# Hashed attention and two feed-forward layers on one core: constant-tile matmuls put into TensorE's order, and a new table of order and engines

## The chip, the core and the metric

The kernel runs on one core of a Trainium2 chip. The core has five instruction streams that run side by side and meet at semaphores: TensorE (PE; its weight loads are listed as PEld), VectorE (DVE), ScalarE (ACT), GpSimd (POOL), and SyncE (SP), which here only issues DMAs. Each engine takes its instructions strictly in the order in which they are written. The metric is the device time of one execution in microseconds (us). TensorE's clock has two levels, 1.2 and 2.4 GHz; the profile gives the granted clock as a share of the upper one, so 0.5 is the lower level, and a number between is a mix of both over a stretch.

## The reference

```python
# attention: batch 2, 8 heads, 768 positions, head size 64, 6 hash bits
q_bits, k_bits = (q @ proj > 0), (k @ proj > 0)      # 6 bits make a bucket
mask   = q_bucket[:, :, :, None] == k_bucket[:, :, None, :]
scores = where(mask, q @ k.T / 8, -1e9)
attn   = softmax(scores)                             # exp(s - max) / (sum + 1e-9)
x = (attn @ v) -> [1536 tokens, 512]
# first layer, 512 -> 2048 -> 512
h = x @ w_in;  g = where(h >= 1, h, where(h <= -1, 0, (h + 1)**2 / 4));  x = g @ w_out
# second layer, same sizes, other weights
h = x @ w_in2; g = h - tanh(h);  y = g @ w_out2
```

The weights arrive as 64-bit floats, everything else as 32-bit floats.

## The kernel before, in words

**Attention** is cut into 96 softmax tiles (48 for each batch), one for 128 query rows of a head against all 768 keys. For a tile, PE makes the scores in two pairs of matmuls (`emit_s`, L435 and L439) into the PSUM tile `ss` (in the first quarter also `mm`); the second pair adds the hash bits in such a way that unequal buckets sink. DVE takes the row maximum (`soft`, L453) and two tiny numbers from it (L456), ACT takes the exponential (L457). The result `p` is split into two 16-bit halves `phl` (a copy, L462, on ACT; a subtraction, L463 on POOL or L464 on DVE), transposed by a DMA into `pt` (L468), or, for three of the head pairs, on PE (`turn`, L512), and multiplied with `v` on PE (`pv`, L550 and L540). The hash bits come from small matmuls into the PSUM tile `pb` (`q_bits` L340 and L341, `k_bits` L326 and L327, `first_k` L309 and L310), which DVE reads (L344, L330, L313). `pb` also takes the spread-out reciprocals of the softmax sums (`scale_l`, L490), the transposes in later tiles, and the largest `v` (L355). There is one `pb`, a PSUM bank of 512 columns of which the kernel uses 384; in the second half of the tiles there is also one `ss` alone.

**The layers** work on 128x512 pieces of weights. A piece is loaded (512 KB, `w<-in_w`), narrowed from 64 to 32 bits (ACT L662; DVE L663, L664, L666, all into `wr`), and split into a high part `wh` (a copy, L227) and a low part `wl` (a subtraction, L233 on POOL or L234 on DVE). Three matmuls of 384 columns each (high x high, high x low, low x high) make up one product (`mats`, L709, 3072 matmuls in all). The results `tmp` are activated (L728 to L733), split again into `gh` and `gl`, and summed in `accs` (L750 to L759). The matmuls of the layers begin during attention, as soon as the first four head pairs are there, and go on alone once attention is over.

**Order and engine.** The code hands some 2000 operations to a `Plan`, each with the engines that can do it: `copy_hi` (L227) may be ACT or DVE, `sub_lo` (L233 POOL, L234 DVE) POOL or DVE, and so on. The table `SCHEDULE`, a packed list of numbers, says in which order the operations are written and which engine takes each (`unpack`, `emit`). Within an engine that order is final. Waits between engines are put in by the framework from the tiles that an instruction reads and writes. Costs that stand beside an operation in the code are not used when the kernel is built.

Of the kernel before, what the change touches and what calls it, by code (L numbers as in the profile page):

```python
# [19 lines left out]
SCHEDULE = (  # L20
    "c-rk&Yj9Q775>)V`<#8wx#vD}-#3q&<lf}oyvT#_N&-RvdCAil1PddT3ZkGwkO&M9d6ic|XsrkYXm|(|Q40e|oeH8I+wqS-svT#n){Zl6wbSX3PJgxgMuCcf"
    "B!E??*~!dVXPv#jyI$W~8?gq`A$cKu5SYj{4i0EbAgcZ~5IWCO3g#2%!3`URZt4bfU5gYsijYhuL=gGo5N9?6M#W5*348F+pnBV&`%q*gvDWRE!slF(tHa?>"
    "l{moKyosO}{ylMWLx($xSv%qmA<iIRq`<<`ixV16jz`1<XKe^}v~m=O9KqBXNj^cgGSBXBQa$=g$o^Fk^cmPkZ$N!cZLKKP{I#e|3GgA@sIRXFr6`>Sij&p6"
    "3VkOgYFI%zV)0mY3^_=aBT<UN5Kt8G7X^?A=lip=@&Z|$BNFkZJjJ0x<_@^y@tj=Lx$+T<Mx7BvZNY6q)Id1w2}y+D4B#IHc|0oz+1c=tCk%Ig!0-RSk!8OR"
    "#|OU`c>i4<kzqI!EC5HmKmu>&c{DQ{#2q@!YVABIdX`7{=_pQf77B%&_-paUf5ve0qfe3_n&uxH3!NW-Xu^^AUY_y0Tu5KDjK}g2e=us~A}0qThCqx*5#lV!"
    "oMe$@x$<0OC{wLS2%(S})cnS@N8zi1*L(L|9h2S6<NBu?9+hFI(+L7hhiOF+HbdBEXmS`f>2o;$0cN}41RUvf6}Nbi$x9OkFZ;#hmoe!@rZIsR__5ezfl;~R"
    "?_}W-j75W-`Pr^b4d7nB6UcgsoLE_717ueydsKm~C`-wg<<jDl+ETovCBWw(uCYfRU~JYbJa|9x&xm~wn>jX4!_Eyf{SUMjn7X<NE3uwUUdiBEb!nyRA}w{I"
    "b@}2}j9G+wJO*O{=1b^j=i#UZaag>FqX+Txc6P}41V;`_v|-;q+P6pFLwM^s@SpNa&%Dkr{`Ml?VnV!`?T86>=^|b;UQ^ZfO8}g^;X382)<DnOIE+KqQT)A~"
    "jL-0?Z2!x?za6qZwf4(BZ4%F!*rnl5Iuv1^=J*)+$jkBWJIsZ5e&c@Itt$78H}EE2w{XFD?d@8_0K1^$S0r8~&R;o2ICBm!sZ^X|FPuEdahxdpy!vq*gzY<E"
    "AGAGf*w5Nrd)afQ!rbGO<}T7DNgdeiP79Y%^f}0W1e0iuq}|Jb7<-a~mOQ<fwJ2AX;0Y}DZf;T4y=Xmi!X_dUkd+dB^>u_6@Ks<d7#1wUV;m2&R<x+r;76A5"  # L30
    "iPhll6>zzhF=1mJG1J2gl~cP~0YB7_59M>qIsZNv%6<o{L!p_Z{K~$-(rUz)R8GxpDdjo56fB71M1ZKa@J_&6)fnfV`*>_{S@z)ECa_5Hln5(h>CuX}1;s_G"
    "Q1UFqr7=Q}x{#+&*K>judby?<vR>wSJUOQ3%6G*z*=XlWBy<>IFFZomqdrwjX$}`pa_(Tt0l>$+Zsr!uX@|MPf%R6g)1n0O^No0+nFmv{92uo3(|9OD1kNcF"
    "`<j}Wu&ZX=hssJm)v5q9rj)+tVH0OfBou4ow6SB67%d9T0y3t>iJD3A(5P#c5ivl=q)B`XmW*dLcQONWWTPD6Lg4=0x@|o>V~A<#1MkK5se_sgr)J}a!c(nH"
    "HYcHvF<vET>|SkrD;w<;5DN*62G586aQ!@cNL}5_s22~^iPZyE-H%oMXD&CejOl1a6|l&7^l_$ocF80B#|N-;o`ap=J{RZAGg}XDRYhX##HKCVw;bQH=_uE*"
    "fvs-`TZ?^Y)7NlqHyA&Wsk)yW!C|*~a0i?R4mkH4_SSQOlY0UuAm2W|3%)mT<kFGjM=l(D=BW1S^EfZ?O8cRE&q5sFe7|b$zi!)mg5mfD^B7ctpFbzgomGT5"
    "bNXij4$k(n7f!%FZXc7+64WSZ*EPkLHqnN?d-$2%T%5)!E}mhEx;xl0V%zX<m5cVxIIyLGZ{D~U8+U`&3#KAMJMc8NBL*3<Hc14rJ}i;7y<nSIl|LV18|M$<"
    "$hu93vg2;7&e<1Tll{~R>~bz&u{FBoIF=tp@(7;P*FoE;Lh<3kRcdC?0??DRycJmHYBgK@_J+kR(pa-_As%0;M&yEJ8s@dHZ1pZ#F6MgJB1Ni2S$KSh5A)%9"
    "SeP!%+2DE5z-))2)(Q=L{)|VUQZsE%OrzPe1(r3<TIvpRJTZf{*kU>?V$GN*;lVM@a6-)lb0%rfG%(h@tprZG8&lN8Twhl=-p|+oYx?N^m}-u6Q%w_Sl0A`O"
    "ymc4Gsrkr8LC}bqyonmw<eB#}G~d@eofgC7{2pM6t?h#)=9*%drOHF1eyDy225AH94Nhv>_v;7N7ls?<(pfHjrRfseTPz((cfW+AuR2j1hgB^tm=${3P<5|5"
    "T%n_&fHRQHQQbWX5%wkoq^m*K!C9@zQDc$vMZI~zb!I2jpo^G!WI!rj=?H282ZWCd3aCv!8xC-jD`$0|Cb?jmx<il}6;4?q%hC>{tyGZ(En(CkSt#=>h~?%Y"  # L40
    "EeJ&;P@f!zL5ZRP4T)skgk(c)Vn71bNP32=-V^UrHrW3FTsebM$jmsK+Y@S=s^TFyCOSr0SulsEFl=P;bfb8Pk!)--hSU$9lrZY8ftE4G>^BptPpJ}}s)c9Y"
    "6N?}uCh1)D6VFruYGQ0OyJI*|-cWATp>!ZCVMvz@N!3)RpmI2+Kgz}eqsL+FC{&F?<?s=eBS)go(4l>hRbD~l9Y}EB;|3B=R89c9i`A5aN>R~(#xzPBF<@|U"
    "f24{^lm&@IMIpw3$IB~`DplKx(tVIZB3aTeiBw@(VG&q<AuCXU&dn#vCM1!F6e1i0f?<RMkzf%1Xeba2sg{l`uh*+gWbnFdWd0ncX}Z+(hmmm@nM<Ieo&lj!"
    "DAZ1vP^?r{tvbAtucyB%Ynk)vU)?Izo6LZU4o%1Vjj*qe*Kw``<?>VFio)oQeOL9L+jkXD(XK<fqW_Y8oyls4RDNZEnN(h>8<e^RqeGKXUKP|vsFuqzvf6nC"
    "s1q&ym-35%U4H8N7s1pr->3uN@-gLn=HhWJz?JX%6+bV#`?;WB7L>Q0S<tyCt_j^W*!Uto86;hN9(t(^%-jyp@rx|8Ewe$Wr3@DxupPeku5at2uLzglsdIfd"
    "@d!6QPF;bs|Iak^uJ3xV>Dy@`eS=}8TLYzD0`@xGyLwme>Rq>~_kCrqP**qE?lw^Bffe6aucw|{OW&Q5LAT=Qx9r+TUoZUE;lkHrGX3va(&MwYh5Pgk(xr<J"
    "UAjp(*@n7rDs`LF)S3Ns?Wyip8FhtzJ6p~TB27KEv|CZXvDtJ3ir*-N)B|t3J#o7zB<evf>AKMLr6f}iDAbjm-9x3D=P`93m2S2d+**}WPhIZndUhLn%a=Lb"
    "Gr6m0&#`Z}t+$TXm9BG<x~uIngmfM8X576Vz|B-o=W)3qz<&S=KC)c"
)


# [65 lines left out]
def lsh_attention_moe_kernel(ctx: ExitStack, tc: tile.TileContext, qT, kT, vR, projR, eye, w1, w2, w3, w4, out, nbits):  # L117
    nc = tc.nc
    B, H, D, S = qT.shape
# [689 lines left out]
    def pump(first):  # L809

        while True:
            n, p = ahead
            if n < NW and (room if raw[n] else n < p + len(WR) and free(n)):
                w_load(n)
                ahead[0] += 1
            elif p < n and free(p) and p - len(WH) < first:
                w_narrow(p)
                w_split(p)
                ahead[1] += 1
            else:  # L820
                return
# [86 lines left out]
```

## Time and profile before

| | us |
|---|---|
| median of 3 runs | 814.67 |
| lowest, highest run | 814.52, 821.42 |
| profiled execution, its own time | 816.48 |
| its span, first to last instruction | 814.7 |
| PE busy in the span | 751.9 (92%) |
| DVE, ACT, POOL busy | 555.3, 517.4, 269.7 |
| mean granted clock of PE | 0.969 |

So 1.8 us of the profiled execution lie around the span. Busy time is the union of an engine's instructions; a PE that is busy at the lower clock does half the work.

### The profile page before, as it was taken

What the parts mean: (1) busy time and instruction counts of PE and PEld (TensorE: products, weight loads), DVE (VectorE), ACT (ScalarE), POOL (GpSimd) and SP (SyncE); (2) the same over time, 40 slices, a digit from 0 to 9 for tenths busy, and PEclk for the clock granted to TensorE, in tenths of its full rate; (3) what the DMA queues carried; (4) which work ended last, traced back from release to release, by engine and by line L of the source; (5) the groups of instructions that cost most, each with busy time, mean ns of one, the idle gap of its engine ahead of it and who ended that gap; (6) DMA issues with size and microseconds to landing.
All of it is one profiled execution on the core that took longest, in us unless ns stands there. A gap on an engine that the chain in (4) does not pass through costs nothing.

```text
span 814.7 us, 12098 instructions
## 1 busy us (share of the span) xinstructions
PE 751.9 (92%) x4344; PEld 686.9 (84%) x4344; DVE 555.3 (68%) x950; ACT 517.4 (64%) x846; POOL 269.7 (33%) x197
## 2 busy tenths in 40 slices
...
GB/s 180 221 210 214 155 173 134 224 203 218 223 205 110 258 217 191 188 171 185 188 199 178 205 142 272 189 180 66 65 66 65 65 56 62 66 67 62 65 39 78
DMA packets 163724, 123.35 MB, mean 151 GB/s; under 512 B 126800, under 2 KB 133712, under 8 KB 163664
## 3 DMA queue, kind: packets, MB, share of 16 engines
...
q8 instruction: 34, 0.56, 0.3%
...
HBM read 71.96 MB, written 19.92 MB: 113 GB/s over the span
## 4 chain that ended last, share of the span: by engine, by line
PE 55%; DVE 4%; ACT 3%; DMA 3%; issue 1%; DVEq 0%; ACTq 0%; POOL 0%; POOLq 0%
PE mm L709 49%; PE pv L550 3%; DMA w<-in_w 2%; PE ss L435 1%; PE ss L439 1%; DVE sm L453 1%; ACT p L457 1%; DVE wr L666 1%; DVE wr L663 1%; DVE wr L664 0%; DMA pt<-phl 0%; DVE accs L759 0%; DVE phl L464 0%; PE pb L490 0%; ACT wh L227 0%
## 5 line engine op out<-in xcount | busy, mean ns | idle before, releaser
L233 POOL TENSOR_TENSOR wl<-wr,wh 128x512 fp32r<-128x512 f32 x85 | 113.4, 1340 | 369.5 <-ACT wh L227 360.6
L227 ACT ACTIVATE wh<-wr 128x512 fp32r<-128x512 f32 x144 | 89.7, 625 | 93.3 <-PE mm L709 82.1
L709 PE MATMUL mm<-xh,wh 128*128 128x384 f32 x512 | 138.7, 341 | 7.0 <-DVE tmp L730 3.9
L709 PE MATMUL mm<-gh,wh 128*128 128x384 f32 x512 | 138.1, 340 | 3.6 <-DVE accs L757 1.7
L709 PE MATMUL mm<-xl,wh 128*128 128x384 f32 x512 | 136.4, 336 | 0.8 <-POOL xl L233 0.8
L709 PE MATMUL mm<-gh,wl 128*128 128x384 f32 x512 | 135.8, 336 | 0.1
L709 PE MATMUL mm<-xh,wl 128*128 128x384 f32 x512 | 135.7, 336 | 0.0
L709 PE MATMUL mm<-gl,wh 128*128 128x384 f32 x512 | 135.7, 335 | 0.0
L457 ACT ACTIVATE p<-ss,sm 128x768 f32<-128x768 f32 x78 | 77.1, 988 | 43.8 <-DVE sm L456 41.2
L709 PEld LDWEIGHTS mm<-xh,wh 128*128 128x128 f32 x512 | 92.5, 189 | 12.4 <-DVE tmp L730 5.1
L709 PEld LDWEIGHTS mm<-gh,wh 128*128 128x128 f32 x512 | 92.3, 188 | 7.5 <-DVE tmp L730 2.9
L453 DVE TENSOR_REDUCE sm<-ss 128x1 f32<-128x768 f32 x82 | 78.2, 953 | 29.1 <-PE ss L439 25.5
L709 PEld LDWEIGHTS mm<-xl,wh 128*128 128x128 f32 x512 | 93.5, 189 | 1.8 <-POOL xl L233 1.8
L709 PEld LDWEIGHTS mm<-gh,wl 128*128 128x128 f32 x512 | 93.2, 188 | 0.4 <-POOL wl L233 0.4
L709 PEld LDWEIGHTS mm<-gl,wh 128*128 128x128 f32 x512 | 93.4, 188 | 0.0
L709 PEld LDWEIGHTS mm<-xh,wl 128*128 128x128 f32 x512 | 93.3, 189 | 0.0
L463 POOL TENSOR_TENSOR phl<-p,phl 128x768 f16<-128x768 f32 x35 | 59.1, 1688 | 70.3 <-ACT phl L462 65.8
L759 DVE TENSOR_TENSOR accs<-mm,accs 128x768 f32<-128x768 f32 x45 | 42.8, 954 | 55.5 <-PE mm L709 55.2
L234 DVE TENSOR_TENSOR wl<-wr,wh 128x512 fp32r<-128x512 f32 x59 | 42.9, 727 | 52.2 <-ACT wh L227 52.0
L227 ACT ACTIVATE gh<-tmp 128x768 fp32r<-128x768 f32 x64 | 53.9, 844 | 33.1 <-DVE tmp L730 18.2
L234 DVE TENSOR_TENSOR gl<-tmp,gh 128x768 fp32r<-128x768 f32 x53 | 51.8, 979 | 29.8 <-ACT gh L227 29.7
L462 ACT ACTIVATE phl<-p 128x768 f16<-128x768 f32 x69 | 57.8, 838 | 4.0 <-DMA pt<-phl 2.9
(162 smaller groups left out, 1192.0 us busy)
## 6 DMA issues: line engine op xcount, KB each, us to landing
...
```

What stands on the lines that cost most here:

```text
L227: ways = [("A", ca, lambda: A.activation(dst, src, AF.Copy)), ("V", cv, lambda: V.tensor_copy(dst, src), 1)]
L233: op([("G", cg, lambda: G.tensor_tensor(dst, src, hi.bitcast(F32), op=ALU.subtract)), ("V", cv, lambda: V.tensor_tensor(dst, src, hi.bitca ...
L234: ("V", cv, lambda: V.tensor_tensor(dst, src, hi.bitcast(F32), op=ALU.subtract), 1)], reads, writes)
L435: T.matmul(ps[:, c, 0:SH], Aq[n][:, i * 128:(i + 1) * 128], a[:, c * SH:(c + 1) * SH], start=True, stop=False)
L439: T.matmul(ps[:, c, 0:SH], Bq[n][:, i * 128:(i + 1) * 128], b_[:, c * SH:(c + 1) * SH], start=False, stop=True)
L453: one("V", 870.0, lambda: V.tensor_reduce(z[:, 0:1], s, axis=AX.XY, op=ALU.max), cell, [c])
L457: one("A", 970.0, lambda: A.activation(halves(p), s, AF.Exp, bias=z[:, 2:3], scale=z[:, 1:2], accum_out=LS[lm][:, lk:lk + 1]), cell + [c], ...
L462: hi = [("A", 730.0, lambda: A.activation(hl[:, 0:S], p, AF.Copy)), ("V", 470.0, lambda: V.tensor_copy(hl[:, 0:S], p), 1)]
L463: lo = [("G", 1600.0, lambda: G.tensor_tensor(hl[:, S:2 * S], p, hl[:, 0:S], op=ALU.subtract)), ("V", 870.0, lambda: V.tensor_tensor(hl[:, ...
L550: T.matmul(ps[j * 64:j * 64 + 64], v[:, kc, a, j, :], PT[n[j]][:, c * KC + kc, :], start=(kc == 0 and i == 0), stop=(kc == KC - 1 and i == 2))
L709: T.matmul(ps[:, s + hf, 0:SH], m[:, kc * 128:(kc + 1) * 128], y[:, hf * SH:(hf + 1) * SH], start=(kc == 0 and i == 0), stop=(kc == 3 and ...
L759: one("V", 870.0, lambda: V.tensor_tensor(a, ps, a, op=ALU.add), [pc], c)
```

## The change

Three things change. First, a constant 128x128 tile `warm` of 16-bit floats is made once on DVE (a copy of the unit matrix, as the fifteenth or so of DVE's instructions), and 65 new operations `spin` of four matmuls each multiply it with itself into the columns 384 to 511 of `pb`, which nothing reads. They have no reads or writes in the plan, and each of the 260 matmuls has a weight load of its own. Second, the table is another one: order and engines differ in nearly every place. Third, a cost beside L490's operation changes, which is not used.

```diff
+SPINS = 65
 SCHEDULE = (
...
+    warm = sb.tile([128, 128], F16, name="warm")
+    WT = PB[0][:, 3 * 128:4 * 128]
...
+    V.tensor_copy(warm, unit)
...
-            one("PE", 406.0, fn, [("rb", 0), ("rb", 1)], ["pb"])
+            one("PE", 640.0, fn, [("rb", 0), ("rb", 1)], ["pb"])
...
+    def spin():
+        for _ in range(4):
+            T.matmul(WT, warm, warm, start=True, stop=True)
+
+    for _ in range(SPINS):
+        one("PE", 300.0, spin, [], [])
+        plan.rows[len(plan.ops) - 1] = 0.7
     plan.emit()
```

Counted in the two built programs, the instructions of the engines move so: ACT 752 to 653, DVE 952 to 1040, POOL 202 to 214, PE 260 matmuls more and otherwise the same. The copies (L227) go from ACT to DVE: `wh` 46 of 144, `gh` 19 of 64, `aq` 7, `bq` 4, `xh` 5, and `phl` (L462) 5. Of these 86 copies 52 stand behind the last row maximum (L453) in DVE's order. Of the subtractions for `phl`, 14 go from DVE to POOL; of those for `gl` 7 go from DVE to POOL, and of those for `xl` 13 come from POOL to DVE. Of the 260 new matmuls, 120 stand ahead of the 29th softmax tile, 60 more ahead of the 48th, 80 between the 48th and the 53rd, and none later. In the new program's waits, the first matmul of a spin waits in 21 places for the DVE or ACT instruction that reads what PE wrote into `pb` before, and 11 reads of `pb` by DVE or ACT wait for a spin that stands between PE's write and the read.

**PE's order where batch 0 goes over into batch 1.** `gh,aq` is the last score tile of batch 0 (the 48th), `ak,aq` the first of batch 1. Before:

```order
L439 MATMUL ss_154<-gl_131,bq_78 128x384 x2
L709 MATMUL mm_153<-xh_137,wh_119 128x384 x2
L709 MATMUL mm_153<-xl_145,wh_119 128x384 x2
L709 MATMUL mm_153<-xh_137,wl_122 128x384 x2
L435 MATMUL ss_154<-gh_126,aq_75 128x384 x2
L439 MATMUL ss_154<-gl_131,bq_78 128x384 x2
L435 MATMUL ss_154<-ak_71,aq_76 128x384 x2
L439 MATMUL ss_154<-bk_73,bq_79 128x384 x2
L490 MATMUL pb_156<-unit,rb_102 128x128 x3
L435 MATMUL ss_154<-ak_71,aq_76 128x384 x2
```

The changed order has the following there (line numbers are 9 higher from here on: L444 and L448 are the scores, L718 is the layers' matmul).

```order
L448 MATMUL ss_154<-gl_131,bq_78 128x384 x2
L718 MATMUL mm_153<-xh_136,wh_119 128x384 x2
L718 MATMUL mm_153<-xl_144,wh_119 128x384 x2
L718 MATMUL mm_153<-xh_136,wl_122 128x384 x2
L718 MATMUL mm_153<-xh_137,wh_119 128x384 x2
L718 MATMUL mm_153<-xl_145,wh_119 128x384 x2
L718 MATMUL mm_153<-xh_137,wl_122 128x384 x2
L444 MATMUL ss_154<-gh_126,aq_75 128x384 x2
L448 MATMUL ss_154<-gl_131,bq_78 128x384 x2
L872 LDWEIGHTS warm
L872 MATMUL pb_156<-warm 128x128
```

Twelve layer matmuls instead of six now stand ahead of the last score tile of batch 0, and behind it 32 matmuls of the constant tile (the last two rows, 32 times over) ahead of the first tile of batch 1. Behind that tile stand 8 more, then L490, then 4 and, past the next hash bits, 8.

**PE's order early, around the hash bits of a query group.** The place is in the first dozen score tiles; `aq` into `pb` (L340 before, L349 now) are the hash bits, which DVE reads. Before:

```order
L439 MATMUL mm_152<-xl_148,bq_78 128x384 x2
L340 MATMUL pb_156<-aq_76,pw_65 128x384
L341 MATMUL pb_156<-aq_76,pw_66 128x384
L435 MATMUL mm_153<-xh_140,aq_75 128x384 x2
L439 MATMUL mm_153<-xl_148,bq_78 128x384 x2
L550 LDWEIGHTS v_0_85
```

Now:

```order
L444 MATMUL mm_153<-xh_140,aq_75 128x384 x2
L499 MATMUL pb_156<-unit,rb_102 128x128 x3
L448 MATMUL mm_153<-xl_148,bq_78 128x384 x2
L872 LDWEIGHTS warm
L872 MATMUL pb_156<-warm 128x128
```

Three more such pairs follow, one spin in all, and then the hash bits (L349 and L350). So a spin stands between L499, whose result ACT reads out of `pb`, and the hash bits: its first matmul waits for ACT's read. Two more spins follow L350, and DVE's read of the bits (L353) waits for one of them.

**DVE's order at the 61st row maximum.** `wr` is a weight piece being narrowed, `bq` the hash bits that a later score tile needs. Before:

```order
L453 TENSOR_REDUCE sm_94<-ss_154 128x1
L456 TENSOR_SCALAR sm_94<-sm_94 128x1 x2
L666 SCALAR_TENSOR_TENSOR wr_116<-w_1_112,wr_116 128x512
L481 TENSOR_SCALAR ls_101<-ls_101,vsm_90 128x6
L663 TENSOR_SCALAR wr_113<-w_0_111 128x512
L483 RECIPROCAL ls_101<-ls_101 128x6
L664 SCALAR_TENSOR_TENSOR wr_113<-w_0_111,wr_113 128x512
L234 TENSOR_TENSOR wl_120<-wr_116,wh_117 128x512
L666 SCALAR_TENSOR_TENSOR wr_113<-w_0_111,wr_113 128x512
```

Now:

```order
L462 TENSOR_REDUCE sm_94<-ss_154 128x1
L465 TENSOR_SCALAR sm_94<-sm_94 128x1 x2
L739 SCALAR_TENSOR_TENSOR tmp_134<-tmp_134,mm_153 128x768
L673 SCALAR_TENSOR_TENSOR wr_114<-w_1_112,wr_114 128x512
L503 COPY rb_102<-pb_156 128x384
L236 CAST wh_118<-wr_113 128x512
L675 SCALAR_TENSOR_TENSOR wr_114<-w_1_112,wr_114 128x512
L353 TENSOR_SCALAR bq_79<-pb_156,cb 12x384
L243 TENSOR_TENSOR wl_121<-wr_113,wh_118 128x512
```

Two operations that ACT had before now stand on DVE between two row maxima: the copy out of `pb` (L503) and the copy that makes `wh` (L236). The read of the hash bits (L353) stands behind both.

## Rows read from the trace of the kernel before

**Rows 1.** The page's first part: busy us (share of the span) and instructions of each engine.
```profile
PE 751.9 (92%) x4344; PEld 686.9 (84%) x4344; DVE 555.3 (68%) x950; ACT 517.4 (64%) x846; POOL 269.7 (33%) x197
```

**Rows 2.** Windows of the span: from:to, length, busy us (instructions) of PE, PEld, DVE, ACT, POOL, granted clock, DMA share, GB/s.
```profile
8.00:20.00 12.00, 6.92 (x23) 4.71 (x22) 9.88 (x15) 10.63 (x19) 5.74 (x5) 1.00 0.57 172
20.00:60.00 40.00, 30.70 (x131) 23.74 (x132) 36.10 (x83) 33.90 (x60) 19.70 (x14) 0.71 0.99 211
60.00:90.00 30.00, 23.98 (x153) 16.77 (x151) 26.49 (x54) 23.99 (x44) 6.84 (x6) 0.98 0.62 194
90.00:130.00 40.00, 35.02 (x184) 26.55 (x186) 25.44 (x54) 32.31 (x58) 16.13 (x12) 0.91 0.76 181
130.00:197.00 67.00, 61.37 (x371) 51.59 (x368) 55.44 (x105) 54.98 (x99) 41.88 (x32) 0.97 0.70 187
197.00:216.00 19.00, 11.01 (x49) 7.83 (x49) 13.97 (x29) 9.90 (x17) 5.90 (x4) 0.64 1.02 259
216.00:340.00 124.00, 116.38 (x709) 105.08 (x705) 100.94 (x179) 102.03 (x173) 69.01 (x49) 1.00 0.79 192
340.00:530.00 190.00, 185.66 (x1105) 172.56 (x1106) 168.39 (x287) 128.87 (x212) 60.45 (x42) 0.99 0.78 193
530.00:814.70 284.70, 279.88 (x1630) 277.45 (x1629) 115.74 (x138) 115.16 (x162) 41.70 (x32) 1.00 0.26 71
```

**Rows 3.** The chain that ended last, in order of time: start us, us, what.
```profile
311.73 0.67 PE pb L490 x6
...
543.80 115.68 PE mm L709 x666
...
668.18 141.82 PE mm L709 x816
```

**Rows 4.** PE's timeline at 200 us: start us, us, instruction [idle before <-releaser].
```profile
200.99 1.01 PE L435 MATMUL ss<-gh,aq 128*128 128x384 f32 x2 [2.85 <-ACT p L457]
201.80 0.84 PE L439 MATMUL ss<-gl,bq 128*128 128x384 f32 x2
205.28 1.01 PE L435 MATMUL ss<-ak,aq 128*128 128x384 f32 x2 [2.64 <-ACT p L457]
206.09 0.84 PE L439 MATMUL ss<-bk,bq 128*128 128x384 f32 x2
209.43 1.65 PE L490 MATMUL pb<-unit,rb 128*128 128x128 f32 x6 [2.50 <-ACT rb L486]
210.74 0.99 PE L435 MATMUL ss<-ak,aq 128*128 128x384 f32 x2
211.52 0.84 PE L439 MATMUL ss<-bk,bq 128*128 128x384 f32 x2
```

**Rows 5.** PE's timeline at 97 us, the same two pairs of score matmuls.
```profile
97.36 0.51 PE L435 MATMUL ss<-ak,aq 128*128 128x384 f32 x2
97.70 0.51 PE L439 MATMUL ss<-bk,bq 128*128 128x384 f32 x2
```

**Rows 6.** Waits up to 230 us: who waited for whom, us in total, times, longest.
```profile
DVE sm L453 <- PE ss L439: 12.8, 10, 3.4
```

**Rows 7.** Groups by shape: line engine operation out<-in xcount | busy us, mean ns | idle before <-releasers.
```profile
L227 ACT ACTIVATE wh<-wr 128x512 fp32r<-128x512 f32 x144 | 89.7, 625 | 93.3 <-PE mm L709 82.1 <-issue 4.7 <-DVE wr L666 4.7
L464 DVE TENSOR_TENSOR phl<-p,phl 128x768 f16<-128x768 f32 x34 | 32.4, 952 | 8.6 <-ACT phl L462 6.9 <-issue 1.6
L666 DVE SCALAR_TENSOR_TENSOR wr<-w,wr 128x512 int32<-128x512 int32 x60 | 44.6, 749 | 0.5
L234 DVE TENSOR_TENSOR wl<-wr,wh 128x512 fp32r<-128x512 f32 x59 | 42.9, 727 | 52.2 <-ACT wh L227 52.0
L344 DVE TENSOR_SCALAR bq<-pb,cb 12x384 fp32r<-12x384 f32 x32 | 19.7, 615 | 8.6 <-PE pb L341 7.9
L234 DVE TENSOR_TENSOR aq<-qr,aq 64x384 fp32r<-64x384 f32 x6 | 3.3, 556 | 0.7 <-ACT aq L227 0.6
L197 DVE CAST pw<-tmp 128x128 fp32r<-128x128 f32 x1 | 0.2, 226 | 0.0
```

**Rows 8.** Line L663 by itself: duration ns min/median/max, first and last start us.
```profile
L663 DVE TENSOR_SCALAR wr<-w x60: 401/426/1872, 45.5 to 520.2; 128x512 int32<-128x512 int32 x60
```

**Rows 9.** Timeline of DVE at 283 us, while POOL works.
```profile
283.63 2.15 DVE L666 SCALAR_TENSOR_TENSOR wr<-w,wr 128x512 int32<-128x512 int32 x1
```

**Rows 10.** Timeline of POOL at 283 us.
```profile
283.13 2.09 POOL L463 TENSOR_TENSOR phl<-p,phl 128x768 f16<-128x768 f32 x1 [1.71 <-ACT phl L462]
```

More of the change, by code (lines that the diff above doesn't have):

```diff
@@ L17 @@
 AX = mybir.AxisListType
+SPINS = 65
 SCHEDULE = (
[L21 to L48, printed above, removed]
+    "c-rk)du)~E8GoMl@_p}jJKt%0F70VgdwMx-Y3cn!OE0ug5Gr+omWhs=8X&=V8JSClfCY3S0y+ehh{z=%x|<l83mGhIUXW-ci+51mqDz*|%s-4-X5yZ=OvQ5A"
@@ new lines @@
+    "o{Gub#uF&t_kPd&d!P6BT+9Bd90gV>x-OWe2@vFr#Xn<~qmCnhR7%{z{n{HG8^RW-L@ijVQUMq+&JIRou@3>BU+^hkJ-07D9UuT6WM{jPZp9dz)e3il!2<yh"
+    "83hH^uJ9{Yun<7mzI{r6XN84^<M_Vs1QH3bqlotWP$2@&$;izOBId;7aaxPTY)8t>o4*r=o}Not8CfOq@3XGEzN4dKVjE&_?>f#;{{fgWsgW_Lt7~m-Mc@*q"
+    "Pj{Okc6>^sgI!&dZ2NFW?ZS?ZB<p6ZxYJ~%rG>1eZX%Q*vb?;VERkD_<MTQ?V~IrKfxNsYlgVTwNpe+QUNP2K5FM``h(x2Mxhhmv7A`8TsK^e73Mwi9GPAO>"
+    "jDn(!!t7`~uc9IzhlmL|;v>w=$a8rt*9l~2_XQm%9F9i&v$E=)42Ex1(k92U=w}w@x1Y!?b<i{&6_4BIZ*4QniXMrEVlhPHW8a8IeI{HXcrfVNwryGQ_>?ne"
@@ new lines @@
+    "EdIwGisz6#q!i$L_?mnbgBcL^*~=$gFXO|%y+R~gZ?acR&s)CSgTuJeF~PV(04TM@&+&6qL@6l^i%AJ^?X|A^){U&d;hY=HFhE|5NY5)dUjfk7)djatBEZR$"
+    "+izTd@+6b+^2u%y3^p%byqG9#U~J*SmDmVN8Wz<!;BrUVSMJ%f2iR;@MreJ;Lq^|a;?!0#bITU-TKugzz$O8c5$`*Op4V~59UdOTyYBoI;<}b2M>x-{LX=Xj"
+    "z*`k+`RVdqyK;B!`aYmxh+T*~$TY<Gb=yAsbQ@#$-pi0JWD5|lfx8gruEl4c?OgN0@7EkZj<TO__q*WpE4aV?*TC4}qel-NIz+MZ$tU>C$4@_f@F1E`y+`5y"
+    "bMw@xQ<Ma6zWM(9^0C)Xp8;X-6K}t5oqhv|_m=?R#Yn_7Eel^faUu-cbjn2hc&?C+6h~DKDZnA)kRXN+W@cvUAP)rQ1p>kS-bdi?Wgoy_A@HXU{~QR|XPE1{"
@@ new lines @@
+    "?^^Ht<un6$=N-$+ef9MmMG_95)G#jzMybP}fBw1W=naoaOCAxXiI#yB-CRok6ylTOAD;jo#)C*{<Ue*G7Xtf%zV6xm>~8QLeRMYkC+!x(aLzc5_rrZe=w^95"
+    "BSUg6C%|4?bhoy0m9cK6kq59{=r;yiwrtpdLOikqF%Y=>7Jn<-!q_7ZGQgia*ua-kfEcUxY^F?<13MY4-GNH2+I|~jLP~bk5BYL=i{#=a0es`300}`YUAh!)"
+    "JH##P`u<6rlTT@P-=%g~R72JepthE{G+WEs$|jU`bSweUC?`xPSt!+P@||R?it;RmVTyy2l9J}4A|VoWbqgj>ork<8zp075dZiO1l~{6IcCA}p3=Sj`Av=*^"
+    "mZ4^{DGdz`<SV0HAZBsiEPY>c^lOr?D+>w=cp@R}{5+v}EXIxcY{Ljs_yZk9>i_h^H8o*_gay4owc|JuKr1tcBg+lyWx9xA-b%H>3}RM<laZz=4Bw}kima}V"
```

19 lines of the change are left out of this document (added).

## Prediction, made before the changed kernel ran

> **What bounds the kernel now.** I read the page's busy times first, then windows of the span with busy time and granted clock side by side, then the chain that ended last, then PE's timeline where the windows show PE idle or its clock low. PE is busy 751.9 of 814.7 us [rows 1], far ahead of DVE and ACT. The windows [rows 2] show four stretches with different limits. From 530 us to the end PE is busy all the time at full clock; the chain [rows 3] has 666 layer matmuls in 115.68 us there, 0.174 us each. No order can shorten that: the work behind the last score tile is the same in both kernels (1590 layer matmuls before, 1584 now). From 216 to 530 us PE is busy 302 of 314 us at a clock of 0.99 to 1.00. So from 216 us on PE is the bound, with 12 us of idle time, and whatever reaches 216 us earlier ends earlier. From 8 to 197 us PE is idle 31.0 of 189 us and DVE is the fullest engine for most of it: 36.1 of 40 us from 20 to 60, 26.5 of 30 from 60 to 90. From 197 to 216 us nothing is full: PE is busy 11.0 of 19 us at a clock of 0.64. There the work is one round after another: scores on PE, row maximum on DVE, exponential on ACT, and only then the next scores, since there is one `ss`. PE waits 2.85, 2.64 and 2.50 us ahead of its work [rows 4].
>
> The low clock has a price in these windows: busy time times what is missing of the clock. That is 30.7 x 0.29 = 8.9 us from 20 to 60, 24.0 x 0.02 = 0.5 to 90, 35.0 x 0.09 = 3.2 to 130, 61.4 x 0.03 = 1.8 to 197, 11.0 x 0.36 = 4.0 to 216, and 185.7 x 0.01 = 1.9 later, together 20.3 us [rows 2]. It counts only where somebody waits for PE.
>
> **The change part by part.**
>
> *The clock from 197 to 216 us.* The four score matmuls of a tile take from 200.99 to 202.64, 1.65 us, at the lower level, behind a wait of 2.85 us; the same four take 97.36 to 98.21, 0.85 us, at the upper one [rows 4, 5]. Three such tiles lie in the stretch: 2.4 us. L490's six passes take 1.65 instead of 0.67 us [rows 3, 4]: 1.0 more. With the rest of PE's work the window gives 4.0 us. PE is the bound right behind it, so all of it would come off the end. The new order has 52 matmuls of the constant tile in these waits and 28 more just behind, and 12 instead of 6 layer matmuls ahead of the first wait, which puts 6 x 0.174 = 1.0 us of real work into an idle place. I take -5.0, with -1.0 if the clock falls all the same and a little over -5 as the other end.
>
> *The clock from 20 to 130 us.* Here 12.6 us of PE's time is lost to the clock, but DVE is fuller than PE. The bound from above is 12.6; from below it is nothing. DVE's row maxima wait for PE's scores 12.8 us in all up to 230 us, in 10 waits [rows 6], most of it a round trip that a faster PE shortens only in part. I take a little over a quarter of 12.6: -3.5. The Trainium skill speaks against so much (TensorE: Matmul & The Clock Gate, What's actually happening): it puts the loss from the clock's ramp at under 1% of a typical kernel's span. By that, both clock terms could bring no more than about 8 us, as an estimate from that page; the rows give 20.3 us, 2.5% of this span, since the clock falls many times here, and my two terms take 7.5 of it.
>
> *DVE's load early.* Up to the 24th row maximum DVE gets rid of four subtractions over 768 columns (two for `phl`, one for `v`, one for keys) at 0.95 [rows 7], of a short one at 0.56, and of the narrowing of two weight pieces (twice 0.43 by L663's median [rows 8] and two steps of 0.75 [rows 7]): 8.2 us. It gains three subtractions at 0.56, a read of bits at 0.62, small ones at 0.4, and four copies. A copy from 32 bit to 32 bit on DVE is in the trace only at 128 columns, 226 ns [rows 7]; the nearest wide row of one input is L663, 401 to 426 ns at 512 columns when undisturbed. I price copies at 0.3 us for 384 columns, 0.43 for 512 and 0.55 for 768: 1.5 us here. Net 8.2 - 2.7 - 1.5 = 4.0. DVE is the fullest engine in 20 to 90 us, so I take -4.0; the ends are 0 (ACT as the true bound, which also loses nine instructions) and -6.
>
> *DVE's load later.* Counted up to the 96th row maximum DVE has 50 instructions more than before: about 34 copies (14.6 us by the prices above), 6 copies out of PSUM at about 0.5, subtractions for `wl`, `xl`, `gl`, `aq` (about 13 net of those dropped), less 15 subtractions for `phl` at 0.95. That is 19 us more by the end of the tiles, so 23 after the 24th; by the same count 12 of it up to the 48th, 15 up to the 72nd, and 5 less in the last 24. DVE's idle time covers it: 14.6 us from 90 to 130, 11.6 to 197, 23 from 216 to 340 [rows 2]. ACT loses as much, and the wait for a copy to cross engines goes. But a copy on DVE can be held up by POOL: L666 took 2.15 us instead of its mean of 0.75 while POOL had an operation of 2.09 us [rows 9, 10], and L663, 0.43 by its median, went up to 1.87 [rows 8]. If one copy in five meets this for 1 us, that is 7 us on DVE, of which I put +2.0 on the path. The 52 copies behind the last tile cost nothing: DVE is busy 116 of 285 us there. If that cover went, they would cost some 22 us.
>
> *The spins themselves.* 260 matmuls of 128 columns. From above, a pass of L490 with its weights: 0.67 / 6 = 0.112, so 29 us. From below, by columns from the layer matmul: 0.174 x 128 / 384 = 0.058, so 15 us. PE's idle time from 8 to 216 us is 39.0 us [rows 2], so they fit, but not freely: PE works in order, and a spin that runs into the moment when the scores could start delays them. Besides, they write to the same tile as the hash bits. 21 of them wait for a read of `pb`, 11 reads wait for a spin; at four to eight matmuls of 0.058 to 0.112 that is 0.23 to 0.9 us a read, some 5 us for the 11, of which half meets a DVE that is full. I take +2.5, with 0 and +8 as ends.
>
> *The order.* The new one has the layer matmuls earlier against the tiles: 78 instead of 51 by the 33rd, 360 instead of 342 by the 57th, 1104 instead of 1014 by the 83rd. Where PE is the bound, that takes from the 12 us of idle time between 216 and 530; I take -2.0.
>
> The sum: -5.0 - 3.5 - 4.0 + 2.0 + 2.5 - 2.0 = -10.0 us. The profiled execution took 816.48 us, 814.7 of span and 1.8 around it, and lies 1.8 above the median of the runs, 814.67. Off that median the forecast is **804.7 us**.
>
> **The rivals.**
>
> *The clock does not hold.* The change doesn't do what it is made for: PE is already 77% busy from 20 to 60 us, and yet the clock is at 0.71, so some short matmuls more need not lift it. Then the -5.0 becomes -1.0 and the -3.5 nothing: -1 - 4 + 2 + 2.5 - 2 = -2.5, 812.2 us. For it: the spins are 0.23 to 0.45 us pieces in waits of two to three. Against it: 32 in one place make up 1.9 us or more.
>
> *Spins hold PE up.* Each of the 21 waits for a reader of `pb`. If the read is itself queued behind a row maximum, it is late by 0.95 + 0.62 = 1.57 us [rows 7], and PE's scores behind the spin with it; 21 of these are 33 us. At 1.0 us each the result is -10 + 22 = +12, 826.7 us. Slower by 1% begins at (10 + 8.1) / 21 = 0.86 us a spin. Against it: the next matmul is often one into `pb` that waits for that read anyway.
>
> *DVE becomes the bound.* From 216 to 530 us DVE is busy 269 of 314 us already, 89% from 340 on [rows 2]. If half of the 34 copies meet POOL for the whole difference, 1.45 us [rows 8], DVE gains 25 us where it has little room: -10 - 2 + 25 is about +13, 827.7 us; slower by 1% begins at some 13 copies. The Trainium skill states the mechanism (SBUF — State Buffer, Who interferes with whom): copies and casts may take a port that DVE shares with GpSimd, and whoever comes second waits out the whole instruction; rows 9 and 10 agree, 2.15 beside 2.09 us.
>
> *All of the clock comes back.* If the early stretch is after all bound by PE's latencies, -3.5 becomes -12.6 and the spins cost nothing: -10 - 9.1 - 2.5 = -21.6, 793.1 us.
>
> **How the numbers follow.** The forecast's case 0.50, with its own range of 796 to 812 from the ends of its terms; clock not held 0.22; spins hold up 0.08; DVE bound 0.09; all of it 0.11. About 1%, 8 us, is what a measurement of this kernel can tell from no change. Of the forecast's case three quarters lie below 806.5, so faster is 0.37 + 0.11 = 0.48, same 0.13 + 0.22 = 0.35, slower 0.17. The range 791 to 823 leaves out some 0.04 below and 0.13 above.
>
> **What would show it.** Right: a granted clock near 1 from 197 to 216 us, scores of 0.85 us there, and the 53rd tile some 8 us earlier than before; from there on the two traces keep their distance to the end. The early term is right if the 24th tile comes 5 us or more sooner, wrong if DVE's idle time there grows instead. Wrong: a clock still near 0.7 in 20 to 60 us; waits of PE's scores behind a spin; copies on DVE of 1 to 2 us; a PE idle for more than 12 us between the 53rd tile and the last.

## The result and the profile after

The changed kernel took 804.34 us (median of 4 runs, 800.99 to 806.18), the kernel before 815.98 on the same chip: a ratio of 0.983 [0.981, 0.986] over the runs, or 13.6 us less [11.5, 15.8]; the two medians by themselves differ by 11.6. The forecast was 804.7 us. The total was right, but by luck: the experiments below show that most of its parts were not.

Busy us (share of the span) and instructions of the kernel after, as in [rows 1]:

```profile
PE 755.5 (94%) x4604; PEld 694.8 (86%) x4604; DVE 607.2 (75%) x1038; ACT 461.8 (57%) x747; POOL 307.5 (38%) x209
```

The windows of the kernel after, with the columns of [rows 2]:

```profile
20.00:60.00 40.00, 29.47 (x158) 21.65 (x159) 34.73 (x72) 30.55 (x55) 22.56 (x15) 0.91 0.80 169
60.00:90.00 30.00, 27.24 (x214) 20.94 (x212) 27.88 (x58) 25.41 (x48) 8.53 (x7) 1.00 0.75 206
90.00:130.00 40.00, 38.76 (x270) 30.80 (x267) 36.19 (x70) 35.00 (x59) 19.62 (x13) 1.00 0.87 201
130.00:197.00 67.00, 59.30 (x379) 48.39 (x378) 59.79 (x121) 53.07 (x94) 30.73 (x22) 1.00 0.87 218
197.00:216.00 19.00, 15.35 (x149) 12.31 (x147) 15.25 (x33) 12.40 (x22) 8.61 (x6) 1.00 1.08 223
216.00:340.00 124.00, 118.98 (x726) 111.02 (x726) 115.51 (x199) 95.47 (x156) 61.35 (x40) 1.00 0.76 185
340.00:530.00 190.00, 185.37 (x1114) 173.81 (x1110) 177.83 (x296) 119.22 (x195) 69.56 (x46) 0.99 0.78 197
```

At first sight this is the change doing what it says: the clock's column stands at 0.91 instead of 0.71 from 20 to 60 us and at 1.00 instead of 0.64 from 197 to 216. The 0.91 is too high, though. This trace has no record of the clock ahead of 28.8 us, and there the column shows 1.00 while a pair of score matmuls takes 1.01 us, as at the lower level in [rows 4]; at the upper one it takes 0.51 [rows 5]:

```profile
22.20 1.01 PE L448 MATMUL ss<-bk,bq 128*128 128x384 f32 x2
```
```profile
20.00:28.80 8.80, 6.61 (x21) 5.29 (x22) 8.00 (x12) 6.02 (x11) 3.92 (x3) 1.00 0.52 133
```

With these 8.8 us at the lower level the clock is 0.80 from 20 to 60 us. (The kernel before has its first record at 13.2 us, so its 0.71 stands.) What is missing of the clock, times busy time, is then 6.61 x 0.5 + 29.47 x 0.09 + 185.37 x 0.01 = 7.8 us, where it was 20.3. And where batch 0 goes over into batch 1, PE's timeline (the place of [rows 4]) looks as forecast:

```profile
195.95 0.62 PE L444 MATMUL ss<-gh,aq 128*128 128x384 f32 x2 [0.87 <-ACT p L466]
196.41 0.50 PE L448 MATMUL ss<-gl,bq 128*128 128x384 f32 x2
196.75 1.96 PE L872 MATMUL pb<-warm 128*128 128x128 f16 x32
199.70 0.62 PE L444 MATMUL ss<-ak,aq 128*128 128x384 f32 x2 [0.98 <-ACT p L466]
200.15 0.51 PE L448 MATMUL ss<-bk,bq 128*128 128x384 f32 x2
201.22 0.94 PE L499 MATMUL pb<-unit,rb 128*128 128x128 f32 x6
```

The four score matmuls take 0.96 us (199.70 to 200.66) instead of 1.65, and the 32 matmuls of the constant tile fill 1.96 us, 0.061 each, of a wait of 2.9.

To see where time was won I counted PE's real work (the spins left out), each kind at its price at the upper clock level, and read off when each kernel had done how much. The changed kernel is 4.9 us behind the old one at the work that the old one has done by 53 us, level at 86, 7.7 us ahead at 118, 3.0 at 197, some 7 at 214, and 10.3 at the end (by the spans, 814.7 and 804.4). So it is not won early, and the largest step lies between 86 and 118 us, where the prediction had nothing but a share of the clock. The scores of the 24th tile even end 3.2 us later (86.3 before, 89.6 now), those of the 53rd 6.8 us sooner (229.0, 222.2). Not all of the 3.2 us need be the kernel's: experiment three below has the same instructions up to there, and in its trace the 24th tile ends at 86.1. Between the scores of the 24th tile and of the 48th, with 228 layer matmuls in both kernels, lie 116.3 us before and 107.4 now. The layers' matmuls alone, in the windows of 96 to 126 us, of the kernel before (first row) and after (second row; PE, PEld, clock, DMA, GB/s):

```profile
96.00:126.00 30.00, 10.07 (x48) 8.78 (x48) 0.94 0.76 167
```
```profile
96.00:126.00 30.00, 15.54 (x78) 13.45 (x78) 1.00 0.96 208
```

Thirty more layer matmuls are done there, 30 x 0.174 = 5.2 us of work, at the same number of tiles (31 by 120 us in both).

### The profile page after: what moved, and what is told of

It is laid out like the page before. It is cut to its first block, busy times and chain, and to the rows that moved or that the text cites. A ratio compares the mean times of both kernels' runs of the same rounds, so it can differ in the third digit from the quotient of the medians.

```text
span 804.4 us, 12604 instructions
## 1 busy us (share of the span) xinstructions
PE 755.5 (94%) x4604; PEld 694.8 (86%) x4604; DVE 607.2 (75%) x1038; ACT 461.8 (57%) x747; POOL 307.5 (38%) x209
## 5 line engine op out<-in xcount | busy, mean ns | idle before, releaser
L242 POOL TENSOR_TENSOR wl<-wr,wh 128x512 fp32r<-128x512 f32 x87 | 119.0, 1372 | 253.7 <-ACT wh L236 151.3
L718 PE MATMUL mm<-xh,wh 128*128 128x384 f32 x512 | 137.5, 339 | 2.3 <-DVE tmp L739 1.3
L718 PE MATMUL mm<-gh,wh 128*128 128x384 f32 x512 | 137.1, 338 | 2.1 <-DVE tmp L739 1.6
L718 PE MATMUL mm<-xh,wl 128*128 128x384 f32 x512 | 136.0, 336 | 0.4 <-POOL wl L242 0.4
L718 PE MATMUL mm<-gh,wl 128*128 128x384 f32 x512 | 135.6, 335 | 0.1
L718 PE MATMUL mm<-gl,wh 128*128 128x384 f32 x512 | 135.6, 335 | 0.1
L718 PE MATMUL mm<-xl,wh 128*128 128x384 f32 x512 | 135.6, 335 | 0.0
L472 POOL TENSOR_TENSOR phl<-p,phl 128x768 f16<-128x768 f32 x46 | 79.1, 1719 | 89.5 <-ACT phl L471 73.5
L236 ACT ACTIVATE wh<-wr 128x512 fp32r<-128x512 f32 x98 | 60.7, 623 | 83.5 <-PE mm L718 70.7
L718 PEld LDWEIGHTS mm<-xh,wh 128*128 128x128 f32 x512 | 92.5, 189 | 5.4 <-DVE tmp L739 2.0
L718 PEld LDWEIGHTS mm<-gh,wh 128*128 128x128 f32 x512 | 92.4, 188 | 5.3 <-DVE tmp L739 2.3
L718 PEld LDWEIGHTS mm<-xh,wl 128*128 128x128 f32 x512 | 93.2, 188 | 1.0 <-POOL wl L242 0.7
L718 PEld LDWEIGHTS mm<-gh,wl 128*128 128x128 f32 x512 | 93.0, 188 | 0.8 <-DVE wl L243 0.7
L718 PEld LDWEIGHTS mm<-gl,wh 128*128 128x128 f32 x512 | 92.8, 188 | 0.7 <-DVE gl L243 0.6
L718 PEld LDWEIGHTS mm<-xl,wh 128*128 128x128 f32 x512 | 93.3, 188 | 0.0
L462 DVE TENSOR_REDUCE sm<-ss 128x1 f32<-128x768 f32 x82 | 78.1, 953 | 7.2 <-PE ss L448 6.0
L242 POOL TENSOR_TENSOR gl<-tmp,gh 128x768 fp32r<-128x768 f32 x18 | 35.5, 1969 | 72.5 <-ACT gh L236 31.4
L471 ACT ACTIVATE phl<-p 128x768 f16<-128x768 f32 x65 | 54.6, 840 | 4.0 <-DMA pt<-phl 1.3
L243 DVE TENSOR_TENSOR gl<-tmp,gh 128x768 fp32r<-128x768 f32 x46 | 47.0, 1024 | 9.1 <-ACT gh L236 8.6
L671 ACT ACTIVATE w<-w 128x512 f32<-128x512 f32 x60 | 40.2, 670 | 23.2 <-DMA w<-in_w 23.0
```

Of the source, the lines that this page charges most:

```text
L236: ways = [("A", ca, lambda: A.activation(dst, src, AF.Copy)), ("V", cv, lambda: V.tensor_copy(dst, src), 1)]
L242: op([("G", cg, lambda: G.tensor_tensor(dst, src, hi.bitcast(F32), op=ALU.subtract)), ("V", cv, lambda: V.tensor_tensor(dst, src, hi.bitca ...
L243: ("V", cv, lambda: V.tensor_tensor(dst, src, hi.bitcast(F32), op=ALU.subtract), 1)], reads, writes)
L462: one("V", 870.0, lambda: V.tensor_reduce(z[:, 0:1], s, axis=AX.XY, op=ALU.max), cell, [c])
L471: hi = [("A", 730.0, lambda: A.activation(hl[:, 0:S], p, AF.Copy)), ("V", 470.0, lambda: V.tensor_copy(hl[:, 0:S], p), 1)]
L472: lo = [("G", 1600.0, lambda: G.tensor_tensor(hl[:, S:2 * S], p, hl[:, 0:S], op=ALU.subtract)), ("V", 870.0, lambda: V.tensor_tensor(hl[:, ...
```

## The experiments

All ratios are to the kernel before on the same chip in the same session, with 95% intervals. "Spins" are the operations of four matmuls of the constant tile.

**One: order and engines without spins.** The spins stay in the table, but write no instruction.

```diff
     def spin():
-        for _ in range(4):
+        for _ in range(0):
             T.matmul(WT, warm, warm, start=True, stop=True)
```

> The changed kernel with its order and engines, but none of the 260 constant matmuls. My sum had the clock bring 7.5 us and the spins cost 2.5, so without them 5 us are lost: about 809.5 us, a ratio of 0.992 to the kernel before, and the clock low again near 200 us (0.6 to 0.7). If the order alone makes the gain (rival), 804 us, 0.985, whatever the clock does. If the spins are all of it, 814 to 816 us, 1.00.

800.61 us, ratio 0.983 [0.978, 0.987]: all of the gain, without one spin.

**Two: the spins without order and engines.** The order and engines of before, with the 65 spins put where the changed kernel has them: behind the same score tile and the same number of PE's operations after it.

```diff
     def emit(self):
         out, engine = self.order()
+        todo, t, k = list(SPIN_AT), 0, 0
         for i in out:
+            if engine[i] == "PE":
+                while todo and todo[0] <= (t, k):
+                    todo.pop(0)
+                    self.spin()
...
```

> The kernel before with its own order and engines, and the 65 spins put in at the places that they have in the changed kernel, counted by score tiles and by PE's operations since. By my sum 5 us less than before: 810 to 811 us, ratio 0.994, clock above 0.9 from 197 to 216 us. If the order alone makes the gain, no gain or a loss of a few us from PE's extra work and the reads of pb: 815 to 820 us. If the spins are all of it, 804 us.

827.22 us, ratio 1.014 [1.011, 1.017]: 11.5 us slower, outside all three expectations. PE's timeline at the transition, in this kernel (its line numbers are others: L450 and L454 are the scores, L506 spreads the reciprocals, L878 is the spin):

```profile
208.75 0.62 PE L450 MATMUL ss<-gh,aq 128*128 128x384 f32 x2 [2.48 <-ACT p L473]
209.21 0.51 PE L454 MATMUL ss<-gl,bq 128*128 128x384 f32 x2
209.56 3.56 PE L878 MATMUL pb<-warm 128*128 128x128 f16 x32
213.08 0.62 PE L450 MATMUL ss<-ak,aq 128*128 128x384 f32 x2
...
217.00 1.65 PE L506 MATMUL pb<-unit,rb 128*128 128x128 f32 x6 [2.48 <-ACT rb L502]
...
219.63 0.99 PE L450 MATMUL ss<-ak,aq 128*128 128x384 f32 x2
```

The spins do fill the wait here, and tile follows tile as before: 208.75 to 213.08 is 4.33 us, where [rows 4] have 4.29. But the price of 32 is 3.56 us, not 1.96, since they run at the lower level themselves; behind the next scores it is back (1.65 for L506, 0.99 for the scores); and the 24.96 us that the spins take between 8 and 240 us have to come from somewhere. By PE's real work this kernel is 2.3 us behind at 53, 6.5 at 118, 8.1 at 197, 10.6 at 214 and 12.8 at the end: it loses a little everywhere. Its clock from 20 to 60 us is higher than before, 0.83 against 0.71 (0.81 with the 1.9 us ahead of its first record at the lower level):

```profile
20.00:60.00 40.00, 30.34 (x174) 22.79 (x172) 33.43 (x77) 32.21 (x57) 20.14 (x14) 0.83 0.98 199
```

So in this stretch some of the clock came back and no time with it, while 4.77 us of its PE time went to spins.

**Three and four: only the first 45 spins, only the last 20** (those between the 48th and the 53rd tile), each with the changed order and engines.

```diff
             if i >= first:
                 n += 1
+                if not (n <= 45):
+                    continue
```

> The changed kernel with only the first 45 spins, those ahead of the 48th score tile. The stretch near 200 us is left without them: by my sum the 4 us of that clock term are lost, 808 us, ratio 0.990; the progress up to the 40th tile is that of the changed kernel. If the late spins do nothing, 804 us. If the late spins cost PE time that the clock does not give back, 802 us.

> The changed kernel with only the last 20 spins, those behind the 48th score tile. By my sum the first 45 bring 3.5 us of clock and cost most of 2.5, so their loss is worth 1 to 2 us: 805 to 806 us, ratio 0.987. If the early clock matters more than I thought (the 12.6 us that the rows before allow), up to 812 us, 0.995. If the early spins only hold up reads of pb, 802 us.

800.78 us, 0.982 [0.979, 0.984], and 801.09 us, 0.983 [0.979, 0.988]. With all spins 0.983, with the early, with the late, with none 0.982 or 0.983: whatever they bring or cost in the new order lies within some 4 us of nothing. (One trace against another misleads here: the profiled execution of the changed kernel was the longest of its four, 806.18 us, that of experiment one the shortest, 798.05.)

**Five: one matmul in a spin instead of four, in the old order.**

```diff
-        for _ in range(4):
+        for _ in range(1):
```

> The order and engines of before with the 65 spins at the places of the changed kernel, but one matmul of the constant tile in each instead of four (65 instead of 260; four of them cost 1.4%, 11 us). If the spins cost by the time that they take on TensorE (22.8 us for 260): a quarter of it, ratio 1.002 to 1.005. If they cost by the waits on the shared PSUM tile, which one matmul brings as four do: 1.010 to 1.015.

819.3 us, ratio 1.002 [1.000, 1.005]. About 2 us for 65, 11.5 us for 260: the price goes with the number of matmuls, so with PE's time. Waits for readers of the shared `pb`, as many with one matmul as with four, would have left it near 1.01. A reader's own wait for a spin does shrink with the number of matmuls, but in the trace of experiment two these waits come to 3.2 us in all, against 11.5 us lost. In the changed kernel they come to 4.8 us, and the waits of spins for readers to 8.5; the largest of each (who waited for whom, up to 230 us; total, times, longest):

```profile
DVE bq L353 <- PE pb L872: 2.5, 3, 1.2
PE pb L872 <- DVE bq L353: 2.3, 4, 0.7
```

**Six and seven: the table cut at the 33rd tile.** No spins; the one order and its engines up to that tile, the rest of the work in the other order.

```diff
+        head = new[:new.index(self.sec[32]) + 1]
+        mine = set(head)
+        engine = [new_engine[i] if i in mine else old_engine[i] for i in range(len(self.ops))]
+        return head + [i for i in old if i not in mine], engine
```

> The changed order and engines, without any matmul of the constant tile, up to the 33rd score tile; from there the order and engines of before. Theory A (the gain is made before 130 us, where the old order leaves DVE 25.4 us busy in 40, and is merely kept afterwards): the trace is some 10 us or more ahead of before at 118 us and at the end; ratio 0.983 to 0.988. Theory B (the gain comes from the transition at 200 us and from the layers' matmuls that stand earlier behind it): ratio 0.995 to 1.005.

> The reverse: order and engines of before up to the 33rd score tile, the changed ones behind it, no matmul of the constant tile. Theory A: ratio 0.993 to 1.0, at most some 5 us gained, those behind 197 us. Theory B: ratio 0.983 to 0.988.

814.64 us, 0.997 [0.994, 1.000], and 816.9 us, 0.997 [0.993, 1.000]: neither half seems to hold the gain. But the cut spoils the test. By PE's work the first of the two is 12.3 us ahead at 130 us and only 2.5 ahead ten later: the new order has done 27 layer matmuls more by the 33rd tile, and the old order's next tiles, robbed of them, run one behind the other, with little on PE between and waits ahead of them (PE's timeline, L487 the scores, L392 the hash bits):

```profile
125.95 0.62 PE L487 MATMUL ss<-xh,aq 128*128 128x384 f32 x2 [1.30 <-ACT p L510]
...
130.43 0.62 PE L487 MATMUL ss<-xh,aq 128*128 128x384 f32 x2 [1.60 <-ACT p L510]
...
135.33 0.66 PE L392 MATMUL pb<-aq,pw 128*128 128x384 f32 x1 [2.86 <-ACT pt L573]
```

**Eight and nine: the cut at the 48th tile.** There the two orders have done the same work but for seven operations.

```diff
-        head = new[:new.index(self.sec[32]) + 1]
+        head = new[:new.index(self.sec[47]) + 1]
```

> The changed order and engines (no matmul of the constant tile) up to the 48th score tile, the last of batch 0; from there those of before. At this tile the two orders have done the same work but for 2 operations that only the changed one has done and 5 that only the old one has; at the 33rd tile these were 29 and 6, 12 of the 29 on TensorE, so that the earlier splice handed the old order a stretch without layer work. Theory A (the gain is made by the changed first half as a whole and is kept): some 10 us ahead at 118 us and at the end, ratio 0.983 to 0.988. Theory C (the two splices at the 33rd tile gained nothing because the gain is not in any one part): ratio above 0.995.

> The reverse: order and engines of before up to the 48th score tile, the changed ones from there, no matmul of the constant tile. Theory A: only what the second half brings, 2.5 us at 214 us and another 2 by the end: ratio 0.993 to 0.998. Theory C: above 0.995 as well, so it is the sum of this run and the last that tells: by A their losses against before add up to about 16 us, by C they do not.

New up to the 48th tile: 806.54 us, 0.987 [0.980, 0.993]. New from there: 812.64 us, 0.994 [0.991, 0.996]. The two gains, 1.35% and 0.62%, add up to 1.97%, against 1.75% [1.33, 2.17] for both halves together. Theory A holds: some two thirds of the gain, 11 us, lie in the first half, 5 us in the second, and both stay.

**Ten: new only up to the 16th tile** (some 60 us). The same edit, with `self.sec[15]`.

> The changed order and engines, no matmul of the constant tile, up to the 16th score tile only (about 60 us). My prediction's term for a lighter DVE up to the 24th tile, 4.0 us, would show here as a ratio near 0.996. If the gain comes from the stretch 60 to 120 us, where layer matmuls are put into TensorE's waits, there is nothing here: 0.998 to 1.002.

819.49 us, 1.002 [0.999, 1.006]. So the first half's gain is made between the 16th and the 48th tile. By the tiles' times most of it lies behind the 24th: from the scores of the 24th tile to those of the 48th the kernel of experiment one takes 106.1 us, the kernel before 116.3. What happens there is seen in PE's timeline before (first fence, the 27th and 28th tiles) and without spins (second, the 29th and 30th, at about the same time):

```profile
98.39 0.51 PE L439 MATMUL mm<-gl,bq 128*128 128x384 f32 x2
98.91 0.88 PE L512 MATMUL mm<-unit,p 128*128 128x128 f32 x6
101.81 0.95 PE L435 MATMUL ss<-ak,aq 128*128 128x384 f32 x2 [2.02 <-ACT p L457]
102.55 0.84 PE L439 MATMUL ss<-bk,bq 128*128 128x384 f32 x2
```
```profile
100.85 0.51 PE L448 MATMUL ss<-bk,bq 128*128 128x384 f32 x2
101.21 0.33 PE L718 MATMUL mm<-xh,wh 128*128 128x384 f32 x1
...
104.68 0.34 PE L718 MATMUL mm<-xh,wl 128*128 128x384 f32 x1
104.85 0.51 PE L444 MATMUL ss<-ak,aq 128*128 128x384 f32 x2
```

Before, PE stands 2.02 us until ACT has the exponential, and then works at the lower level. Now 21 layer matmuls fill the round trip, and the next scores follow at the upper level without a wait. The weights are not what lets it: three pieces are narrowed and split by 72.2 us before and by 81.5 now. What is there sooner is the layers' input. `pv` of the fourth head pair ends at 99.6 us instead of 114.5, and the low part of its result is made on DVE and no longer on POOL (before, then without spins):

```profile
116.39 1.02 POOL L233 TENSOR_TENSOR xl<-rb,xh 128x384 fp32r<-128x384 f32 x1
```
```profile
100.95 0.56 DVE L243 TENSOR_TENSOR xl<-rb,xh 128x384 fp32r<-128x384 f32 x1
```

From the fourth piece on the weights come sooner too (`wl` at 103.9 us instead of 119.5). How much of the gain each of these brings was not tested. The old order left DVE the time for both: it was busy 25.4 of 40 us from 90 to 130 [rows 2] and is 36.8 now (the windows without spins):

```profile
90.00:130.00 40.00, 37.68 (x234) 30.93 (x234) 36.80 (x71) 35.10 (x63) 18.43 (x14) 1.00 0.87 205
130.00:197.00 67.00, 54.94 (x303) 44.50 (x302) 59.05 (x121) 50.89 (x89) 33.45 (x23) 0.95 0.90 226
197.00:216.00 19.00, 15.48 (x89) 11.60 (x90) 15.64 (x33) 15.04 (x25) 8.15 (x6) 0.90 0.85 204
```

By 120 us this kernel has done 78 layer matmuls (30 before) and 32 tiles (31). By 197 us the layer work is level again, 228 to 222, since both orders place 228 ahead of the 48th tile; but 49 tiles are done instead of 46. What was put into idle places early is out of the tiles' way later.

**Eleven and twelve: order and engines apart**, no spins.

```diff
+        return new, old_engine      # eleven
+        return old, new_engine      # twelve
```

> The changed order, but every operation on the engine that it had before; no matmul of the constant tile. If the order is what counts: ratio 0.983 to 0.988, as without the spins alone. If the choice of engines is what counts (copies from ACT to DVE, so that ACT's exponentials come sooner): 0.995 or above. If the two hang together, since the order was laid out for these engines: above 1.

> The order of before, with each operation on the engine that the change gives it; no matmul of the constant tile. If engines count by themselves: ratio 0.985 to 0.99. If the order counts: 0.998 to 1.01, since copies then stand on DVE ahead of row maxima in places that were not laid out for them.

890.13 us, 1.089 [1.085, 1.093], and 855.05 us, 1.046 [1.042, 1.050]. Each half of the table alone is far slower than either whole. The third expectation for eleven was right: the two hang together. For twelve I had expected 1.01 at most, which missed. In the new order with the old engines PE's scores wait 7.4 us for ACT's exponentials (216 to 530 us; who waited for whom), where the kernel before has 0.6 and that without spins 1.6. That is a small part of the 73 us lost, and ACT's waits for DVE, 35.1 us, do not tell the slow kernel from the fast: without spins they are 34.4. So that the halves don't fit together is shown, and where most of the time goes is not:

```profile
ACT p L507 <- DVE sm L506: 35.1, 21, 5.1
PE ss L484 <- ACT p L507: 7.4, 8, 3.7
```

## Why the total was right and its parts were not

*The clock from 197 to 216 us, -5.0: seen, but not the spins' doing.* Every sign that the prediction named is there: clock 1.00, scores at the upper level, the 53rd tile 6.8 us sooner, and some 4 us won between 197 and 214 us by PE's work. But without spins the same stretch wins 2.9 us (10.1 ahead, then 13.0) at a clock of 0.90, and taking the last 20 spins out leaves the ratio where it was. By place and not by time, from the scores of the 48th tile to those of the 53rd, with 24 layer matmuls in each, the traces take 26.4 us before, 25.3 with all spins, 24.3 with the first 45, 24.8 with the last 20 and 25.8 with none. So the full clock was not worth 5 us there: a tile still waits for the round trip, 4.29 us from scores to scores before [rows 4] and 3.75 now. The twelve layer matmuls ahead of the last tile, which I gave 1.0 us, shorten that wait by themselves to 1.02 us (2.85 in [rows 4]). The step that failed is the conclusion from a sign that two causes share.

*The clock from 20 to 130 us, -3.5: not borne out.* The clock rose from 0.71 to 0.80 from 20 to 60 us, but without spins it is 0.87 there, and the 16th and the 24th tile came 1.8 and 3.2 us later in this trace. Spins took 4.25 us of PE's time from 20 to 60 us, 3.16 to 90 and 3.09 to 130. The Trainium skill (TensorE: Matmul & The Clock Gate, What's actually happening) puts the clock's ramp at under 1% of a typical span; I set its rule against the rows' 2.5% and followed the rows. The rows were right on the clock and did not say what it was worth, nor who would give it back. The loss is 7.8 us in the kernel after and 8.1 without spins, so the order had already brought back what I gave to the spins; in the traces of experiments three and four it is 4.4 and 13.9, and the ratio is 0.982 or 0.983 in all four.

*DVE's load early, -4.0: the load did not fall.* Up to its 24th row maximum DVE is busy 74.8 us before, 78.0 now and 75.8 without spins: what it sheds comes back as instructions that take longer, some of them beside POOL. Without the early spins that row maximum still ends sooner, at 84.9 to 86.5 us in four traces, where the old order has it at 88.6 to 89.4 in three. So the order does win some 3 us by then, through shorter waits of DVE (9.1 us idle instead of 14.6), and the early spins cost them again: it ends at 87.2 and 90.6 us in two traces with the same instructions up to there. The new order up to the 16th tile alone brings nothing. One of the longer instructions is a subtraction of keys, 0.94 us without spins and 2.28 here (DVE, then POOL):

```profile
22.50 2.28 DVE L243 TENSOR_TENSOR xl<-krs,xh 64x768 fp32r<-64x768 f32 x1
```
```profile
22.32 1.65 POOL L472 TENSOR_TENSOR phl<-p,phl 128x768 f16<-128x768 f32 x1 [1.70 <-ACT phl L471]
```

*DVE's load later, +2.0: prices right, cost hidden.* The guessed prices of copies, 0.43 and 0.55 us, are 0.422 and 0.559 by the medians, and some do run into POOL (the 1890 ns beside a POOL instruction of 1743):

```profile
L236 DVE CAST wh<-wr x46: 413/422/1890, 155.1 to 771.1; 128x512 fp32r<-128x512 f32 x46
L236 DVE CAST gh<-tmp x19: 549/559/2148, 223.6 to 786.1; 128x768 fp32r<-128x768 f32 x19
```

By the means (520 and 673 ns) that is 4.5 + 2.2 us over all 65, less than the 7 I had. My 0.5 us for a copy out of PSUM on DVE stood in no row; the two of `rb` take 0.55. PE does not see it: from 216 to 530 us it is idle 9.6 us instead of 12, with DVE busy 293.3 of 314. Behind the last tile the cover held as well: the chain is one run of PE there. No run took these copies apart, so that the cost is hidden is read from PE's idle time, not shown.

```profile
536.02 264.44 PE mm L718 x1524
```

*The spins themselves, +2.5: the unit was right, the sum belongs to the order.* 0.061 us each at the transition lies at the lower bound. In the new order they cost nothing that can be measured, in the old one 11.5 us, more than the upper end of 8. The waits on `pb`, out of which I made my price, are not what they cost there.

*The order, -2.0: this term was mis-sized, and carries the result.* Order and engines together give 14.3 us [10.9, 17.7]. I looked for their gain only in PE's 12 us of idle time from 216 us on. The count that would have told me more was in the prediction: 78 layer matmuls instead of 51 by the 33rd tile, 27 x 0.174 = 4.7 us of work put into a stretch where PE waits, about half of the 10 us that the order wins between the 24th tile and the 48th. I gave the idle time of 8 to 216 us to spins alone, although real work in the same places both ends the wait and is done.

So the sum of -10.0 holds -6.0 for the spins and their clock, 1.0 of it for layer matmuls (measured: nothing, within 4 us) and -4.0 for order and engines (measured: -14.3). Two errors of opposite sign made a good forecast, and that was luck.

*The rivals.* The clock did hold from 197 to 216 us. Spins holding PE up is real in the old order (1.4%), by their time on PE and not by `pb`. DVE did not become the bound (its limit for slower by 1% is some 14 copies by its own numbers, not 13). "All of the clock comes back" gave 793 us; 12.5 of the 20.3 us came back, 12.2 of them without any spin as well, and with the spins 22.8 us of PE's time went out for them.

*What stays open.* How much of the order's gain is clock: it lowers the loss from 20.3 to 8.1 us while it fills the waits, and no run did the one without the other. And whether a few of the 65 spins pay: the differences are below what these runs resolve. The kernel without any is simpler, and no slower.
